# Sliding-window attention and a slotted MoE on one core: part of a weight read by the sync queue, and a request moved

## The chip, the cores and the metric

The kernel runs on one core of one Trainium2 chip. A time is the device time of one execution in microseconds. The kernel before was timed 13 times: the median is 183.29 us, the lowest 182.49 and the highest 183.64.

## The reference

Inputs are q, k and v of shape (8 batches, 8 heads, 576 positions, 64), and the MoE's `phi` (512 x 32), `w1` (8 experts, 512 x 1024) and `w2` (8 experts, 1024 x 512), all fp32. Two stages follow each other.

- Attention: scores are `q k^T / 8`. Heads 0 to 3 see the last 32 positions, heads 4 to 7 every fourth of the last 128 ("dilated"). After a softmax over the visible positions the result is multiplied by v. With the heads side by side this gives x, 4608 rows of 512.
- Soft MoE: `logits = x @ phi`. A softmax over the 4608 rows forms 32 slot inputs out of x, four for each expert. Every expert computes `relu(s @ w1) @ w2` on its four slots. A softmax over the 32 slots of each row mixes the 32 slot outputs into that row of the output, 4608 x 512 in fp32.

So w1 and w2 (16.8 MB each in fp32) are read once for 32 rows of work, q, k and v are 9.4 MB each, and the output is 9.4 MB.

## The kernel before

All tensors are computed in fp16. Every load and every store is a DMA issued by POOL (GpSimd), and the DMA converts: loads read fp32 and write fp16, stores read fp16 and write fp32. The order of the instructions of each engine is the program's order (`manual_schedule`), with no planner.

**The batches.** A prologue requests the first inputs and prepares masks. Then ten steps b = 0 to 9 follow, each made of `slot0`, `slot1` and `slot2`. Step b does the scores, exp and attention-times-v of batch b, transposes raw q and k of batch b+1 on DVE (`qk_plain`, L233, and `qk_dil`, L242), and finishes batch b-1: it transposes x (`back_xT_plain`, `back_xT_dil`) and computes the logits (`back_logits`, whose exp on ACT, L409, goes into the tile ET at columns 576 (b-1) and up). `back_erow` and `back_u` of batch b-2 add up the slot inputs.

**The loads.** Raw q and k of batch b+2 are requested in `slot0(b)` (`load_qk`, L132) and v of batch b+2 in `slot1(b)` (`load_v`, L146 for the first 512 positions and L149 for the last 64). `spread_v` copies part of v on DVE (L201) and part on POOL (L204, L208); it stands ahead of `load_v` in the order of POOL. Between these, `weights(b, g)` requests half an expert's w1 at a time (`load_w1(e, i)`, L212, 256 rows of 4 KB, 512 KB once converted) and near the end w2 (`load_w2`, L216 for experts 0 to 5). Experts 6 and 7 are read in halves of 256 columns (L224): first the left half of both, then the right half of both, eight DMAs in all.

**The tile ET** has 128 partitions and 4672 columns of fp16. It is set to zero in `slot0(0)` by DVE (L559), and column 576 b and up is written by ACT when batch b's logits are done, in `slot2(b+1)`. Columns from 2560 on are thus not used until `slot2(5)`.

**The prologue's order on POOL.** Raw q and k of batch 0 in two parts (four requests, L137), then five selects that build `ident` and `masks` (L483), `load_v(0)`, the select that builds `orders` (L493), `load_qk(0, 1)`, `load_qk(1, 1)`, `load_v(1)`, and phi (L505). On DVE the copy L506 waits for the masks and is followed by the first transposes of q and k.

**The end.** `slot_out(half, experts)` multiplies by w2 (L706) and copies 256 columns of slot outputs to `so_sb` (L714). `combine(half, pair)` makes 256 rows by 256 columns of output: two matmuls with ET (L722), a scaling by ACT in two passes (even pairs, L734) or by DVE in one (odd pairs, L738), and one store by POOL (L744). `combine_full(pair)` does 256 rows of all 512 columns (L755, L757, L761, stores L768). The order is: half 0 of w2 for all experts; eight pairs of half 0, with w2's half 1 of expert 6 after the sixth; half 1 of expert 7; then ten full pairs, with the eight pairs of half 1 between the last ones.

Of the kernel before, what the change touches and what calls it, by code (L numbers as in the profile page):

```python
# [44 lines left out]
NH = DMODEL // 2  # L45
# [4 lines left out]
def kernel(  # L50
# [75 lines left out]
    def load_qk(ti, b, groups=None):  # L126
        ten = (q, k)[ti]
        if (ti, b) not in raw:
            raw[(ti, b)] = raw_pool.tile([128, 2, PJ * D], FP16, name=f"raw{ti}_{b}", tag=f"raw{ti}")
        t = raw[(ti, b)]  # L130
        if groups is None:
            nc.gpsimd.dma_start(  # L132
                out=t, in_=ten[b].rearrange("(g h) (p j) d -> (h p) g (j d)", g=2, j=PJ)
            )
        else:
            for g in groups:
                nc.gpsimd.dma_start(  # L137
                    out=t[:, g, :],
                    in_=ten[b, 4 * g : 4 * g + 4].rearrange("h (p j) d -> (h p) (j d)", j=PJ),
                )  # L140

    def load_v(b):
        slab = fix.tile([128, V_SLAB], FP16, name=f"vs_{b}", tag=f"vs{b % 2}")
        sa, sb = (slab[:, 2048 * i : 2048 * i + 2048].rearrange("a (h n) -> a h n", h=H) for i in range(2))
        vstage[b] = (sa, sb)
        nc.gpsimd.dma_start(  # L146
            out=sa, in_=v[b, :, 0:512, :].rearrange("h (a r) d -> a h (r d)", r=DIL)
        )
        nc.gpsimd.dma_start(  # L149
            out=sb[0:LEFT], in_=v[b, :, 512:S, :].rearrange("h (a r) d -> a h (r d)", r=DIL)  # L150
        )
# [57 lines left out]

    def load_w1(e, i):  # L210
        src = moe_w1[e].rearrange("(c p) f -> p c f", p=128)
        nc.gpsimd.dma_start(out=w1t[e][:, 2 * i : 2 * i + 2, :], in_=src[:, 2 * i : 2 * i + 2, :])  # L212

    def load_w2(e, half=None):
        if half is None:
# [242 lines left out]
    def prologue():  # L458
        load_qk(0, 0, (0,))
        load_qk(1, 0, (0,))  # L460
        nc.vector.memset(masks, 0.0)
        nc.vector.memset(ones, 1.0)
        nc.vector.memset(orders[0:32], 1.0)
        for i in range(2):
            nc.vector.memset(kTp[i][:, S : S + 64, :], 0.0)
            nc.vector.memset(kTd[i][:, S : S + 80, :], 0.0)
            nc.vector.memset(qTd[i][:, S : S + 16, :], 0.0)
            nc.vector.memset(vP[i][:, :, :, D : D + 1], 1.0)
            nc.vector.memset(vP[i][TAIL:128, 4, :, :], 0.0)
            nc.vector.memset(vD[i][:, :, :, D : D + 1], 1.0)  # L470
            nc.vector.memset(vL[i][:, :, :, D : D + 1], 1.0)
        load_qk(0, 0, (1,))
        load_qk(1, 0, (1,))
        left = masks[:, W1:].rearrange("p (u c) -> p u c", c=LEFT)
        band = (
            (ident, ones, [[1, 128]], 0, -1, ALU.is_equal, 0.0),
            (masks[:, 0:WQ], masks[:, 0:WQ], [[1, WQ]], 0, -1, ALU.is_ge, MASKED),
            (masks[:, 0:WQ], masks[:, 0:WQ], [[-1, WQ]], WINDOW - 1, 1, ALU.is_ge, MASKED),
            (left, left, [[0, 5], [1, LEFT]], 32, -1, ALU.is_ge, MASKED),
            (left, left, [[0, 5], [-1, LEFT]], -1, 1, ALU.is_ge, MASKED),  # L480
        )
        for dst, src, pattern, base, mult, op, fill in band:
            nc.gpsimd.affine_select(  # L483
                out=dst,
                in_=src,
                pattern=pattern,
                base=base,
                channel_multiplier=mult,
                compare_op=op,
                fill=fill,  # L490
            )
        load_v(0)
        nc.gpsimd.affine_select(  # L493
            out=orders[0:32],
            in_=orders[0:32],
            pattern=[[-1, DIL], [1, 128]],
            base=0,
            channel_multiplier=-DIL,
            compare_op=ALU.is_equal,
            fill=0.0,  # L500
        )
        load_qk(0, 1)
        load_qk(1, 1)
        load_v(1)
        nc.gpsimd.dma_start(out=phi_raw, in_=moe_phi.rearrange("(p l) s -> p l s", l=4))  # L505
        nc.vector.tensor_copy(out=masks[:, WQ:W1], in_=masks[:, 0:TAIL])  # L506
        qk_plain(0, 0)
        qk_plain(1, 0)
        nc.vector.memset(emask, 1.0)
        for i in range(1, 4):  # L510
            nc.vector.tensor_copy(out=orders[32 * i : 32 * i + 32], in_=orders[0:32])
        for part in range(2):
            qk_dil(0, 0, part)
        qk_dil(1, 0, 0)
# [5 lines left out]
    def weights(b, g):  # L520
        if b < B - 2:
            if g == 1 or b > 0:
                load_w1(*next_w1.pop(0))
        elif b == B - 2:
            if g == 0:
                while next_w1:
                    load_w1(*next_w1.pop(0))
                load_w2(0)
                load_w2(1)
            else:  # L530
                slab_weights(4, "vs0", V_SLAB)
                load_w2(4)
        elif g == 0:
            raw_pool.release()
            pool = tc.alloc_tile_pool(name="w2b", bufs=1, side="right")
            late_pools.append(pool)
            for e in (2, 3):
                w2t[e] = pool.tile([128, 8, DMODEL], FP16, name=f"w2_{e}", tag=f"w2_{e}")
                load_w2(e)
        else:  # L540
            slab_weights(5, "vs1", V_SLAB)
            load_w2(5)
            slab_weights(6, "qk0", QK_SLAB)
            slab_weights(7, "v0", V_SLAB)
            for half in range(2):
                for e in HALVED:
                    load_w2(e, half)

    def slot0(b):
        att, b1, b2, b3 = b < B, b - 1 >= 0 and b <= B, 2 <= b < B + 2, b + 1 < B  # L550
        if att:
            qk_dil(1, b, 1)
            emit_scores(b, 0)
            if b + 2 < B:
                load_qk(0, b + 2)
                load_qk(1, b + 2)
            weights(b, 0)
        if b == 0:
            nc.vector.memset(ET, 0.0)  # L559
            nc.vector.memset(siTm, 0.0)  # L560
            nc.vector.tensor_reduce(
                out=halves, in_=orders[:, 0, 0:TAIL], axis=mybir.AxisListType.X, op=ALU.add
            )
            nc.vector.tensor_copy(
                out=emask[:, NE - 1, :], in_=halves.broadcast_to([128, N_SLOTS])
            )
        if b1:
            emit_av(b - 1, "d", 0)
            emit_norm(b - 1, "d", 0)
        if b2:  # L570
            back_erow(b - 2)
        if b1:
            emit_av(b - 1, "d", 1)
            emit_norm(b - 1, "d", 1)
            back_xT_plain(b - 1, 0)
        if att and b > 0:
            order_v_plain(b)
        if b == 1:
            order_phi()
        if b1:  # L580
            emit_av(b - 1, "d", 2)
            emit_norm(b - 1, "d", 2)
            back_xT_plain(b - 1, 1)
        if b2:
            back_u(b - 2)
# [129 lines left out]

    psum_f = tc.alloc_tile_pool(name="psum_f", bufs=4, space=bass.MemoryType.PSUM)

    def combine(half, pair):
        fp = psum_f.tile([128, 2, NH], FP32, name=f"f{half}_{pair}", tag="f")
        r0 = 256 * pair  # L720
        for k in range(2):
            nc.tensor.matmul(  # L722
                fp[:, k, :],
                ET[:, r0 + 128 * k : r0 + 128 * k + 128],
                so_sb[:, NH * half : NH * half + NH],
                start=True,
                stop=True,
                skip_group_check=True,
            )
        ot = out_pool.tile([128, 2, NH], FP16, name=f"ot{half}_{pair}", tag=f"ot{half}", bufs=NSPLIT // 2)  # L730
        if pair % 2 == 0:
            for k in range(2):
                blk = 2 * pair + k
                nc.scalar.activation(  # L734
                    out=ot[:, k, :], in_=fp[:, k, :], func=AF.Copy, scale=rrow[:, blk : blk + 1]
                )
        else:
            nc.vector.tensor_tensor(  # L738
                out=ot,
                in0=fp,  # L740
                in1=rrow[:, 2 * pair : 2 * pair + 2, None].broadcast_to([128, 2, NH]),
                op=ALU.mult,
            )
        nc.gpsimd.dma_start(  # L744
            out=out[r0 : r0 + 256, NH * half : NH * half + NH].rearrange("(k p) n -> p k n", k=2),
            in_=ot,
        )
# [74 lines left out]
```

## Time and profile before

| | |
|---|---|
| median of 13 executions | 183.29 us |
| profiled execution, its own time | 183.64 us |
| span in its trace (first to last instruction) | 181.9 us |
| PE busy | 144.2 us, 79% |
| DVE busy | 106.6 us, 59% |
| ACT busy | 90.7 us, 50% |
| POOL busy | 83.4 us, 46% |
| moved by DMA, counted at the destination | 40.75 MB, mean 224 GB/s |
| read from and written to HBM | 61.93 MB and 9.44 MB, 392 GB/s |

The span is divided by the page into 40 slices. PE is the busiest engine, and between 24 and 112 us its slices are nearly all at nine tenths; yet in the row of the DMA engines every slice but the first is at nine tenths too, to the very end. In the last 24 us only output is written. A line of the timeline gives start, duration, engine, source line, operation, and in brackets how long the engine had been idle and what ended that. Issuing instructions of DMAs are listed under POOL with the time that they hold POOL; the transfer itself comes later.

### The profile page before, as it was taken

What the parts mean: (1) busy time and instruction counts of PE and PEld (TensorE: products, weight loads), DVE (VectorE), ACT (ScalarE), POOL (GpSimd) and SP (SyncE); (2) the same over time, 40 slices, a digit from 0 to 9 for tenths busy, and PEclk for the clock granted to TensorE, in tenths of its full rate; (3) what the DMA queues carried; (4) which work ended last, traced back from release to release, by engine and by line L of the source; (5) the groups of instructions that cost most, each with busy time, mean ns of one, the idle gap of its engine ahead of it and who ended that gap; (6) DMA issues with size and microseconds to landing.
All of it is one profiled execution on the core that took longest, in us unless ns stands there. A gap on an engine that the chain in (4) does not pass through costs nothing.

```text
span 181.9 us, 5572 instructions
## 1 busy us (share of the span) xinstructions
PE 144.2 (79%) x2464; PEld 86.6 (48%) x2464; DVE 106.6 (59%) x231; ACT 90.7 (50%) x163; POOL 83.4 (46%) x117
## 2 busy tenths in 40 slices
PE   0557987999999999999999999999879475787000
PEld 0224544746646746746746746757344263232000
DVE  4788785676884984984984984536040202499100
ACT  2053365748566766766766766765201204698000
POOL 7953642633535345345283715621101110998830
PEclk9999998798799999999999999998556968799755
DMA  4999999999999999999999999999999999999997
GB/s 61 197 164 215 196 210 205 212 209 203 212 209 206 211 211 203 212 210 202 215 207 204 211 211 213 217 214 215 214 212 216 200 196 168 298 397 408 408 407 181
DMA packets 31303, 40.75 MB, mean 224 GB/s; under 512 B 1584, under 2 KB 18992, under 8 KB 31280
## 3 DMA queue, kind: packets, MB, share of 16 engines
q0 software_dynamic: 31280, 40.41, 119.4%
q8 instruction: 19, 0.31, 0.6%
q14 instruction: 4, 0.03, 0.0%
HBM read 61.93 MB, written 9.44 MB: 392 GB/s over the span
## 4 chain that ended last, share of the span: by engine, by line
PE 43%; DMA 32%; ACT 8%; issue 5%; POOL 4%; DVE 3%; POOLq 1%
DMA w<-in_moe_w_dram 23%; PE lg L405 8%; PE o_p L336 7%; PE sa L279 6%; ACT p L290 6%; DMA raw<-in_q_dram 5%; PE sa L268 5%; PE sb L268 4%; DMA out_dram<-of 4%; PE u L447 3%; PE rd L386 2%; PE vb L162 2%; PE va L162 2%; PE rp L374 2%; ACT of L757 1%
## 5 line engine op out<-in xcount | busy, mean ns | idle before, releaser
L290 ACT ACTIVATE p<-sa 128x960 f16<-128x960 f32 (+2 forms) x24 | 21.4, 891 | 31.3 <-PE sb L279 30.7
L336 PEld LDWEIGHTS <-p 128*128 128x128 f16 (+2 forms) x544 | 19.7, 99 | 12.8 <-issue 8.6
L242 DVE STREAM_TRANSPOSE qk<-raw 128x320 uint32<-128x320 uint32 (+1 forms) x32 | 21.6, 679 | 0.3
L233 DVE STREAM_TRANSPOSE qk<-raw 128x576 uint32<-128x576 uint32 x16 | 20.0, 1251 | 2.7 <-DMA raw<-in_q_dram 1.5
L290 ACT ACTIVATE p<-sb 128x960 f16<-128x960 f32 (+2 forms) x24 | 21.2, 885 | 0.0
L208 POOL COPY v<-v 32x1024 f16<-32x1024 f16 x8 | 8.3, 1036 | 27.9 <-DVE v L201 19.3
L268 PE MATMUL sa<-masks,ident 128*128 128x480 f16 (+2 forms) x48 | 14.5, 388 | 6.3 <-POOL masks L483 4.8
L405 PE MATMUL lg<-xTd,phi 128*128 128x288 f16 x32 | 18.3, 659 | 0.0
L279 PEld LDWEIGHTS <-qk 32*128 32x128 f16 x832 | 12.3, 98 | 12.3 <-issue 9.3
L279 PE MATMUL sa<-qk 32*128 32x160 f16 (+4 forms) x416 | 16.2, 215 | 2.0 <-DVE qk L233 1.9
L336 PE MATMUL o_p<-v,p 128*128 128x65 f16 (+1 forms) x288 | 16.7, 203 | 0.8 <-ACT v L171 0.7
L268 PEld LDWEIGHTS <-ident 128*128 128x128 f16 x96 | 9.2, 106 | 16.8 <-issue 7.3
L224 POOL DMA_DIRECT2D w<-in_moe_w_dram x8 | 6.0, 746 | 24.4 <-DMA w<-in_moe_w_dram 21.7
L279 PE MATMUL sb<-qk 32*128 32x160 f16 (+4 forms) x416 | 16.3, 215 | 0.0
L358 DVE TENSOR_TENSOR xd<-o_d,rc_d 128x448 f16<-128x448 f32 (+1 forms) x24 | 14.4, 602 | 0.8
L358 DVE TENSOR_TENSOR xp<-o_p,rc_p 128x448 f16<-128x448 f32 (+1 forms) x24 | 14.4, 602 | 0.8
L744 POOL DMA_DIRECT2D out_dram<-ot x16 | 11.5, 719 | 6.7 <-PE f L722 6.7
L268 PE MATMUL sb<-masks,ident 128*128 128x480 f16 (+2 forms) x48 | 14.4, 386 | 0.2 <-ACT p L290 0.2
L212 POOL DMA_DIRECT2D w<-in_moe_w_dram x16 | 11.6, 728 | 3.2 <-DMA w<-in_moe_w_dram 2.2
L162 PE MATMUL va<-vs,orders 32*128 32x256 f16 (+1 forms) x96 | 12.1, 289 | 1.0 <-ACT p L290 1.0
L409 ACT ACTIVATE ET<-lg 128x288 f16<-128x288 f32 x16 | 6.6, 411 | 12.2 <-PE lg L405 12.0
L738 DVE TENSOR_TENSOR ot<-f,rrow 128x512 f16<-128x512 f32 x8 | 5.5, 688 | 12.0 <-PE f L722 11.9
(97 smaller groups left out, 272.3 us busy)
## 6 DMA issues: line engine op xcount, KB each, us to landing
w<-in_moe_w_dram POOLq DMA_DIRECT2D x16, 512.0 KB, 14.6
w<-in_moe_w_dram POOLq DMA_DIRECT2D x6, 1024.0 KB, 26.5
out_dram<-of POOLq DMA_DIRECT2D x10, 512.0 KB, 6.0
vs<-in_v_dram POOLq DMA_DIRECT2D x8, 512.0 KB, 10.5
out_dram<-ot POOLq DMA_DIRECT2D x16, 256.0 KB, 4.3
raw<-in_q_dram POOLq DMA_DIRECT2D x7, 576.0 KB, 13.3
raw<-in_k_dram POOLq DMA_DIRECT2D x7, 576.0 KB, 13.4
w<-in_moe_w_dram POOLq DMA_DIRECT2D x8, 256.0 KB, 23.9
```

The source lines that it names most:

```text
L162: nc.tensor.matmul(o.rearrange("p (h d) -> p h d", h=4), l, st[:, 0:4, D * r : D * r + D], start=(r == 0), stop=(r == DIL - 1), skip_group ...
L208: nc.gpsimd.tensor_copy(out=vL[b % NV][0:32, :, :, 0:D], in_=vD[b % NV][96:128, :, :, 0:D])
L212: nc.gpsimd.dma_start(out=w1t[e][:, 2 * i : 2 * i + 2, :], in_=src[:, 2 * i : 2 * i + 2, :])
L233: nc.vector.transpose(out=dst, in_=src)
L242: nc.vector.transpose(out=o, in_=i)
L268: nc.tensor.matmul(sps[h // 2][:, h % 2, 0:n], ident, bias[g], start=True, stop=False, skip_group_check=True,)
L279: nc.tensor.matmul(sps[h // 2][:, h % 2, c0 : c0 + w], kt_[32 * h : 32 * h + 32, k0 : k0 + 128, tt], qt_[32 * h : 32 * h + 32, q0 : q0 + w ...
L290: nc.scalar.activation(out=pt, in_=sps[ab][:, :, 0:n], func=AF.Exp, scale=SCALE)
L336: nc.tensor.matmul(o[p0 : p0 + np_, n, :], l, rr, start=(k == 0), stop=(k == len(jobs) - 1), skip_group_check=True,)
L358: nc.vector.tensor_tensor(out=x.rearrange("p t (h d) -> p (t h) d", h=4)[0:nq, u0:u1, :], in0=o[0:nq, 0:n, 0:D], in1=rc[0:nq, 0:n, None].b ...
L405: nc.tensor.matmul(lp, phi4[:, kc].rearrange("p c s -> p (c s)"), rhs, start=(kc == 0), stop=(kc == 3))
L744: nc.gpsimd.dma_start(out=out[r0 : r0 + 256, NH * half : NH * half + NH].rearrange("(k p) n -> p k n", k=2), in_=ot,)
```

## The change

Four things are edited.

- `load_w1(3, 0)` leaves out rows 0 to 127 of expert 3's w1. These are read by 16 DMAs on the sync queue (SP), each of 8 rows, as fp32, into columns 2560 to 4607 of ET seen as fp32 (128 x 1024). They are issued in `slot0(3)`, after a memset of two columns by DVE (`side_load`).
- In `slot0(5)` POOL converts the 128 x 1024 values into w1's tile and sets the columns of ET to zero again (`side_cast`).
- In the prologue `load_v(0)` goes ahead of the five selects, and `load_qk(0, 1)` ahead of the select of `orders`.
- `combine(0, 0)` becomes two calls of the new `combine_one`, each for 128 rows with one matmul, one scaling (ACT for the first, DVE for the second) and one store.

```diff
     def load_w1(e, i):
         src = moe_w1[e].rearrange("(c p) f -> p c f", p=128)
-        nc.gpsimd.dma_start(out=w1t[e][:, 2 * i : 2 * i + 2, :], in_=src[:, 2 * i : 2 * i + 2, :])
+        c0 = 2 * i + (e == SIDE_E and i == 0)
+        nc.gpsimd.dma_start(out=w1t[e][:, c0 : 2 * i + 2, :], in_=src[:, c0 : 2 * i + 2, :])
+
+    SIDE_E, SIDE_C0 = 3, 2560
+    side = ET[:, SIDE_C0 : SIDE_C0 + 2048].bitcast(FP32)
+
+    def side_load():
+        nc.vector.memset(ET[:, SIDE_C0 : SIDE_C0 + 2], 0.0)
+        for p in range(0, 128, 8):
+            nc.sync.dma_start(out=side[p : p + 8], in_=moe_w1[SIDE_E, p : p + 8, :])
+
+    def side_cast():
+        nc.gpsimd.tensor_copy(out=w1t[SIDE_E][:, 0, :], in_=side)
+        nc.gpsimd.memset(ET[:, SIDE_C0 : SIDE_C0 + 2048], 0.0)
...
         load_qk(1, 0, (1,))
+        load_v(0)
         left = masks[:, W1:].rearrange("p (u c) -> p u c", c=LEFT)
...
-        load_v(0)
+        load_qk(0, 1)
         nc.gpsimd.affine_select(
...
-        load_qk(0, 1)
         load_qk(1, 1)
...
             weights(b, 0)
+        if b == 3:
+            side_load()
+        if b == 5:
+            side_cast()
...
+    def combine_one(half, blk):
+        fp = psum_f.tile([128, NH], FP32, name=f"f{half}_one{blk}", tag="f")
+        cols = slice(NH * half, NH * half + NH)
+        r0 = 128 * blk
+        nc.tensor.matmul(fp, ET[:, r0 : r0 + 128], so_sb[:, cols], start=True, stop=True)
+        ot = out_pool.tile([128, NH], FP16, name=f"oo{half}_{blk}", tag=f"oo{half}_{blk}")
+        if blk % 2 == 0:
+            nc.scalar.activation(out=ot, in_=fp, func=AF.Copy, scale=rrow[:, blk : blk + 1])
+        else:
+            nc.vector.tensor_scalar(
+                out=ot, in0=fp, scalar1=rrow[:, blk : blk + 1], scalar2=None, op0=ALU.mult
+            )
+        nc.gpsimd.dma_start(out=out[r0 : r0 + 128, cols], in_=ot)
+
     def combine(half, pair):
+        if half == 0 and pair == 0:
+            combine_one(half, 0)
+            combine_one(half, 1)
+            return
```

## The prediction

> **What bounds the kernel now.** I read the slices of the page first, then the queues, then the chain of waits, then the windows.
>
> ```profile
> DMA  4999999999999999999999999999999999999997
> GB/s 61 197 164 215 196 210 205 212 209 203 212 209 206 211 211 203 212 210 202 215 207 204 211 211 213 217 214 215 214 212 216 200 196 168 298 397 408 408 407 181
> ...
> q0 software_dynamic: 31280, 40.41, 119.4%
> ...
> HBM read 61.93 MB, written 9.44 MB: 392 GB/s over the span
> ```
>
> The DMA engines have packets in flight in every slice but the first; POOL's queue q0 carries everything. Bytes are counted at the destination: loads are written as fp16, so 210 GB/s there is 420 GB/s read. The bytes are fixed by the problem, so the span is start-up, bytes over rate, and the places where the rate falls. Four columns of the windows matter here: stretch, length, and at the end DMA share and GB/s.
>
> ```profile
> 9.00:13.00 4.00, 2.66 (x68) 1.18 (x56) 3.47 (x7) 1.83 (x2) 2.57 (x4) 1.00 1.22 155
> 104.00:108.00 4.00, 4.00 (x67) 2.31 (x67) 3.46 (x8) 3.01 (x6) 1.50 (x2) 1.00 1.12 210
> 148.00:152.00 4.00, 2.42 (x52) 1.77 (x43) 0.00 (x0) 0.00 (x0) 0.00 (x0) 0.77 1.45 196
> 152.00:156.00 4.00, 3.53 (x27) 1.94 (x27) 2.08 (x3) 2.73 (x7) 1.67 (x3) 0.66 1.02 149
> 156.00:160.00 4.00, 2.95 (x19) 1.21 (x18) 1.98 (x3) 2.72 (x6) 4.00 (x6) 0.92 1.81 363
> 168.00:172.00 4.00, 0.00 (x0) 0.00 (x0) 0.78 (x2) 0.00 (x0) 4.00 (x6) 0.79 1.64 408
> ```
>
> Two dips: v(0), at 9 to 13 us, and 152 to 156 us, where w2 runs out before the output begins. The end of the chain shows what waits there:
>
> ```profile
> 146.84 10.43 DMA w<-in_moe_w_dram
> 157.32 0.32 PE so L706 x4
> 157.66 0.38 ACT so_sb L714
> 158.08 0.39 PE f L755
> ```
>
> and the timeline shows the first output:
>
> ```profile
> 151.96 0.29 PE L706 MATMUL so<-w,hTm 128*32 128x256 f16 x4 [1.12 <-DMA w<-in_moe_w_dram]
> 152.30 0.37 ACT L714 CAST so_sb<-so 128x256 f16<-128x256 f32 x1 [9.30 <-PE so L706]
> 153.20 2.35 ACT L734 ACTIVATE ot<-f,rrow 128x256 f16<-128x256 f32 x6 [0.53 <-PE f L722]
> 154.33 5.72 POOL L744 DMA_DIRECT2D out_dram<-ot  x8 [6.75 <-PE f L722]
> ```
>
> [...] The trace records each packet, and every engine's 4-byte completion mark. For the last w2 DMA the marks run from 152.6 to 157.0 us: seven engines are done by 153.8, nine between 154.2 and 157.0; the means (153.1 and 155.4) are 2.3 us apart. Earlier the spread was the same kind (3.2 us at 112.6 us), and from 112 to 137 us nearly all engines step at the same 0.305 us per 8 KB read, so a lag, once there, stays. Early engines stand idle until the first store, which waits for the latest engine's share of expert 7's first half. From 154.33 POOL issues one store each 0.715 us without a pause, the 512 KB stores start when that row is done (160.05), and then 408 GB/s sets the end. So the end moves one for one with that latest engine.
>
> [...]
>
> **The side read.** w1(3,0) loses 128 rows. A w1 row is 4 KB read, and 508 such packets started in the 5 us from 104: 16 engines × 5 / 508 = 0.157 us each. Every engine loses 8 of its 16: −1.26 us. Added are 128 rows of 4 KB read and 4 KB written. The trace has no uncast load; output writes at 408 GB/s give 4096 / 25.5 = 0.161 us per packet. Sixteen per engine on 0 to 7: +2.57 us. Net +1.3 us for engines 0 to 7, −1.26 us for 8 to 15: the sum is nil, the relative shift 2.5 us, beside the 2.3 us of lag just measured.
>
> Which engines lag decides the sign, and no view names them. One hint: where two packets begin in the same nanosecond, the records list one first. From 155.6 to 157 us, of 30 such pairs of a store packet (an early engine) and a w2 packet (a late one), 27 list the store first; from 142 to 147 us the early engine is first in 7 of 8. If equal times stand in order of engine number, the late engines have high numbers. I take that, and that the change relieves them.
>
> Gain: at most 1.26 us at the latest engine (half 0: 151.6 to 150.4). The early seven, the last of which finish 3.2 us ahead of the latest, come up 1.3 us and stay below. But at least one of engines 0 to 7 belongs to the nine; if it is one of those 1.4 us behind the last, it becomes the latest after about 0.1 us of gain. I take 0.9; bounds 0 to 1.26.
>
> Bound from above on the cost: [...] From below it is nothing [...]. I take under 1 us, which the slack covers.
>
> **Its other instructions.** The DVE memset of 2 columns is some 0.07 us (the 128x16 memsets of L470), where DVE then idles 0.9 us (before 55.57); queued behind it are normalisations of batch 2. SP's 16 issues: SP has nothing else before the end. Raw tiles of batch 5, requested at 52.5 and 55.0 us, land 13 us later and are transposed at 74.0 and 76.2, so engines late by even 7 us there cost nothing. The w1 issue shrinks from 0.73 towards 0.56 us (128 rows, as L149), hidden.
>
> POOL's cast and memset stand at 83.8 us. L204's 1024 columns take 1.03 us and I take that for the cast; the 2048-column memset is 2.05 us at that pace, less if it is packed; 16 waits of 0.04 us (a semaphore event of L216) add up to 0.7. Together at most 3.8 us, and behind it are these:
>
> ```profile
> 83.79 1.03 POOL L204 COPY v<-vs 16x1024 f16<-16x1024 f16 x1
> 89.24 1.04 POOL L208 COPY v<-v 32x1024 f16<-32x1024 f16 x1 [4.43 <-DVE v L201]
> ```
>
> L208 waits 4.43 us for DVE: that hides it. Without the cover, v(7) would be requested later, and it is needed a batch later. ACT's exp of batch 4 into these columns comes after 91.7 us; the zeros are there by 88. Cost nil.
>
> **v(0) first.** Its two issues (0.94 + 0.56 us) go ahead of five masks selects: v(0) is requested 1.5 us earlier, masks end at 6.8 instead of 5.3, and DVE's copy L506, with the transposes behind it, starts 0.75 us later. DVE waits 0.74 us for raw at 16.79, which absorbs it; without that cover PE would start batch 1 up to 0.75 us late, still 20 us ahead of w2. q(1) is requested 0.6 us sooner, k(1) and v(1) keep their time. On the engines the order stays q, k, v(0), q, k. v(0)'s packets start at 8.75 us, behind k, 2 us after their request; asking sooner doesn't explain away the dip. Were it fixed, 155 would become 197 GB/s: 4 × 42 / 197 = 0.85 us. I take 0; bounds 0 and 0.85 gained.
>
> **combine_one.** Pair 0 of half 0 leaves in two stores. The first needs one ACT pass of 0.42 us instead of two: POOL starts at 153.9 instead of 154.33. Two issues of 0.56 replace one of 0.72, so pair 1 is issued at 153.9 + 1.12 = 155.0 against 155.05. Early engines start 0.5 us sooner, the row ends 0.05 us sooner. Gain 0.05.
>
> **Sum.** −0.9 −0.05 = −0.95 us on this execution (span 181.9, time 183.64, so 1.74 around it): span about 180.95, time 182.7. Its time is 0.35 above the median 183.29; on the median: 182.3.
>
> **Rivals.** (a) [...] Against: at load SBUF takes only half of what the engines read, and the engines run 3 us apart. It decides from about 1.9 us of extra time, where engines 0 to 7, up by 1.3, overtake the latest[...]. (b) *The late engines are 0 to 7.* The order of ties may mean nothing. Then +1.3 − 0.05: 184.5. (c) *It hides.* The 8 rows are spread over all engines after all, or a middle engine becomes the latest: 183.2. (d) *The dip at 9 us goes too:* 182.3 − 0.7 = 181.6.
>
> **Numbers.** Forecast 0.40, (d) 0.08, (c) 0.13, (a) 0.25, (b) 0.14. A difference below 0.2% (0.37 us) can't be told from none here. Faster 0.48, same 0.13, slower 0.39. The forecast's own range is 181.9 to 182.8; the range for 8 in 10 takes in (b), (c), (d) and the lower half of (a): 181.3 to 185.3.
>
> **What would show it.** Right: 149 GB/s at 152 to 156 rises, the first store is issued near 153 us, the last w2 lands near 156. The side rows show as 4 KB packets on an SP queue from about 55 us, landing within 10 us; POOL's L208 still waits on DVE after the cast. [...] side DMAs that take much longer than 10 us, a GB/s dip at 55 to 70 us, w2 later. (b): no dip there, w2 later by about 1.3. (d): 9 to 13 us near 197 GB/s. I am wrong altogether if the w2 landings don't move while the end does.

## The result and the profile after

| | before | after |
|---|---|---|
| median | 183.38 us (48 runs) | 185.12 us (11 runs, 184.49 to 186.00) |
| profiled execution, its own time | 183.64 us | 184.96 us |
| span in its trace | 181.9 us | 183.1 us |
| read from HBM, written | 61.93, 9.44 MB | 61.93, 9.44 MB |

The changed kernel is slower: 1.0096 of before, 95% interval 1.0079 to 1.0114, or +1.8 us where the forecast was −0.95. 185.12 lies inside the range of 181.3 to 185.3, but only because rivals (a) and (b) had been taken in; the forecast itself had the wrong sign. The two profiled executions that are compared below differ by 1.3 us, a little less than the medians.

The page of the changed kernel: slices of the DMA engines, queues, bytes.

```profile
DMA  4999999999999999999999999999999999999996
GB/s 63 194 190 213 200 207 205 214 204 206 213 206 206 229 217 207 212 182 189 212 211 159 200 211 214 215 215 217 210 215 215 208 195 199 328 395 410 406 409 160
...
q0 software_dynamic: 31168, 40.15, 118.0%
q1 hardware_dynamic: 256, 0.52, 1.2%
...
HBM read 61.93 MB, written 9.44 MB: 390 GB/s over the span
```

The queue q1 is new: 128 packets of 4 KB with their marks. The third slice, which holds v(0), is better than before (190 for 164), and so, taken together, are the two slices from about 146 to 155 us (195 and 199 for 196 and 168). Read by these two dips alone, the change works. The windows of the changed kernel (stretch, length, busy time of PE, weight load, DVE, ACT, POOL with counts, then granted clock, DMA share, GB/s; the share adds up the packets' times over the 16 engines, and passes 1 where an engine's packets overlap) say the same, and show two dips that before did not have. First the changed kernel:

```profile
9.00:13.00 4.00, 2.69 (x65) 1.32 (x60) 3.64 (x7) 1.83 (x2) 2.52 (x4) 1.00 1.31 184
80.00:82.00 2.00, 2.00 (x52) 1.18 (x48) 2.00 (x3) 1.86 (x6) 2.00 (x4) 1.00 0.87 162
96.00:98.00 2.00, 2.00 (x19) 0.98 (x17) 1.55 (x5) 1.55 (x3) 2.00 (x4) 1.00 0.90 137
152.00:156.00 4.00, 2.66 (x16) 1.71 (x15) 1.71 (x3) 1.89 (x5) 1.29 (x3) 0.73 1.44 197
```

The same two stretches in the kernel before:

```profile
80.00:82.00 2.00, 2.00 (x12) 0.61 (x14) 1.93 (x4) 0.41 (x1) 0.53 (x1) 1.00 1.14 207
96.00:98.00 2.00, 1.91 (x46) 1.34 (x36) 1.37 (x5) 1.76 (x3) 0.66 (x1) 1.00 1.38 201
```

152 to 156 us moves 197 GB/s for 149, as the prediction wanted, and yet the end is later, because the w2 in front of it comes later. The chain of waits shows the last w2 at 158.23 us (before 157.32):

```profile
120.55 26.92 DMA w<-in_moe_w_dram
147.47 0.28 issue
147.76 10.43 DMA w<-in_moe_w_dram
158.23 0.32 PE so L723 x4
158.57 0.38 ACT so_sb L731
```

and the timeline of the changed kernel the outputs:

```profile
153.21 0.37 ACT L731 CAST so_sb<-so 128x256 f16<-128x256 f32 x1 [6.12 <-PE so L723]
154.71 1.09 POOL L747 DMA_DIRECT2D out_dram<-oo  x2 [6.21 <-DVE oo L744]
155.79 5.01 POOL L779 DMA_DIRECT2D out_dram<-ot  x7
160.91 2.15 POOL L803 DMA_DIRECT2D out_dram<-of  x3
```

`so_sb` comes at 153.21 (before 152.30), the first store at 154.71 (154.33), the first 512 KB store at 160.91 (160.05): +0.9 us from half 0 of w2 to the row of stores, as w2 goes.

The packet records show what no view groups. Of the last w2 DMAs' 512-byte packets, the first engine to begin does so at 144.94 us (before 141.94), the last packet starts at 157.82 (156.88). The first engine came 3.0 us later, the latest 0.9 later. The prediction had +1.3 for the engines with side rows and up to −1.26 for the others: the spread did shrink, but on a base about 2 us too late. Some of that base is the two new dips of this one execution. In it PE ran at half clock for 6.8 us around 30 us and 6.8 us around 48 us (before 3.4 each) and for 3.4 us more at 62 and 76 us, and POOL, which waits for PE's results, reached its sixth L208 at 93.31 us (before 89.24), with the requests behind it. Whether that is the cause of +1.8 in general is one of the questions below. The side read itself began when planned, on the sync queue:

```profile
56.52 9.73 SPq L221 DMA_DIRECT2D ET<-in_moe_w_dram  x16
```

Its packets start between 59.9 and 70.7 us and take 233 ns on average (up to 493), where 172 ns is the unhindered value, that of the first 28. The first 32 begin in four groups of eight with the same spacing, 0.52 us apart (59.89 to 60.15, 60.41 to 60.66, 60.92 to 61.18, 61.44 to 61.69), and a mark of 4 bytes follows each packet, so eight engines take one row each of these DMAs. Which eight they are no record says. The prediction's "engines 0 to 7" is the author's assumption; below they are also called the eight.

### The profile page after: what moved, and what is told of

The parts are those of the page before. It is cut to its first block, busy times and chain, and to the rows that moved or that the text cites. A ratio compares the mean times of both kernels' runs of the same rounds, so it can differ in the third digit from the quotient of the medians.

```text
span 183.1 us, 5612 instructions
## 1 busy us (share of the span) xinstructions
PE 146.5 (80%) x2464; PEld 87.6 (48%) x2464; DVE 106.7 (58%) x233; ACT 90.6 (50%) x162; POOL 86.0 (47%) x120
## 3 DMA queue, kind: packets, MB, share of 16 engines
HBM read 61.93 MB, written 9.44 MB: 390 GB/s over the span
## 4 chain that ended last, share of the span: by engine, by line
PE 46%; DMA 20%; ACT 11%; DVE 6%; issue 5%; POOL 5%; POOLq 1%; DVEq 0%
DMA w<-in_moe_w_dram 20%; PE lg L418 8%; ACT p L303 7%; PE o_p L349 6%; PE sa L292 6%; PE sb L281 5%; PE sa L281 5%; PE rd L399 3%; PE u L460 3%; PE vb L162 2%; PE va L162 2%; DVE qk L255 2%; PE rp L387 2%; ACT of L792 2%; PE o_d L349 1%
## 5 line engine op out<-in xcount | busy, mean ns | idle before, releaser
L281 PE MATMUL sa<-masks,ident 128*128 128x480 f16 (+2 forms) x48 | 15.7, 416 | 7.3 <-POOL masks L497 6.2
L208 POOL COPY v<-v 32x1024 f16<-32x1024 f16 x8 | 8.3, 1036 | 26.5 <-PE sb L292 13.8
L292 PEld LDWEIGHTS <-qk 32*128 32x128 f16 x832 | 12.8, 101 | 12.0 <-issue 10.2
L292 PE MATMUL sa<-qk 32*128 32x160 f16 (+4 forms) x416 | 16.7, 219 | 0.8 <-DVE qk L246 0.7
L237 POOL DMA_DIRECT2D w<-in_moe_w_dram x8 | 6.0, 746 | 21.3 <-DMA w<-in_moe_w_dram 20.5
L281 PE MATMUL sb<-masks,ident 128*128 128x480 f16 (+2 forms) x48 | 15.4, 410 | 0.5 <-ACT p L303 0.5
L370 DVE RECIPROCAL rc_p<-o_p 128x7 f32<-128x7 f32 (+1 forms) x24 | 4.7, 197 | 13.0 <-PE o_p L349 12.5
L132 POOL DMA_DIRECT2D raw<-in_q_dram x7 | 5.0, 720 | 14.4 <-DVE qk L255 12.0
L392 ACT COPY xTp<-rp 128x576 f16<-128x576 f16 x16 | 10.4, 647 | 2.2 <-PE rp L387 2.2
```

The lines of the kernel that those rows point to most:

```text
L208: nc.gpsimd.tensor_copy(out=vL[b % NV][0:32, :, :, 0:D], in_=vD[b % NV][96:128, :, :, 0:D])
L281: nc.tensor.matmul(sps[h // 2][:, h % 2, 0:n], ident, bias[g], start=True, stop=False, skip_group_check=True,)
L292: nc.tensor.matmul(sps[h // 2][:, h % 2, c0 : c0 + w], kt_[32 * h : 32 * h + 32, k0 : k0 + 128, tt], qt_[32 * h : 32 * h + 32, q0 : q0 + w ...
L392: nc.scalar.copy(out=xTp_t[b][:, c, :], in_=rg)
```

## The experiments

The rivals stand against each other as follows. **Neighbours** (rival (a), theory C in the expectations): eight engines that carry 8 neighbouring rows at a time hold one another up, and the cost goes away when the same engines carry rows that lie apart. **Skew** (theory D): 16 more packets on each of the eight engines make one of them the latest, neighbours or not. **Clock and dry spells:** the side read has nothing to do with it, PE is late, and requests with it. **Parts:** the moved v(0) or `combine_one` cost the time. Every ratio is to the kernel before on the same chip.

**One part at a time.** The prologue alone:

```diff
+        load_v(0)            # ahead of the five selects
...
-        load_v(0)
+        load_qk(0, 1)        # ahead of the select of orders
```

> Only load_v(0) and load_qk(0, 1) are moved in the prologue. Theory A (PE is granted half clock more often in the batches, PE gets late, requests come late, the DMA engines run dry): the move fills the DMA dip at 9 to 13 us (155 to about 184 GB/s, as in the changed kernel) and the engines, now ahead, wait for PE; whether the kernel is slower follows the number of half-clock stretches before 112 us, 2 in the kernel before and 6 in the changed one. About 184.5 us if this edit alone brings more of them, 182.7 us if it brings none. Theory B (the side read costs): 182.7 us, faster by 0.6.

Measured: 182.87 us, 0.9976 (0.9957 to 0.9995). Windows and timeline of this kernel:

```profile
9.00:13.00 4.00, 2.70 (x67) 1.32 (x60) 3.64 (x7) 1.83 (x2) 2.52 (x4) 1.00 1.35 193
...
151.03 0.37 ACT L714 CAST so_sb<-so 128x256 f16<-128x256 f32 x1 [7.03 <-PE so L706]
153.27 5.71 POOL L744 DMA_DIRECT2D out_dram<-ot  x8 [7.05 <-ACT ot L734]
...
158.98 2.14 POOL L768 DMA_DIRECT2D out_dram<-of  x3
```

193 GB/s for 155 in the kernel before, and the whole tail about 1.1 us earlier in this execution. The packet records say how: v(0)'s 1152 packets of 512 bytes start at 8.8 us in both kernels, but the last starts at 12.61 instead of 13.59 us; the DMA share of the stretch 9 to 10 us is 1.30 instead of 0.95. So the first packet does not start earlier; what changed is that the engines no longer run empty between these packets. By the medians the part is worth −0.44 us (0.0024 x 183.58).

The side read alone, with `load_w1`, `side_load` and `side_cast` as in the change and nothing else:

```diff
+        if b == 3:
+            side_load()
+        if b == 5:
+            side_cast()
```

> Only the side read on the sync queue with its cast. Theory A: 182.3 to 182.5 us if the half-clock stretches stay at 2, since the late engines are relieved (152 to 156 us near 197 GB/s); about 184 if there are 5 or 6. Theory B (the side read itself costs, by its requests, its cast or its DMAs): about 185 us.

Measured: 185.94 us, 1.0138 (1.0084 to 1.0192). Here the dip at 152 to 156 us stays, and the next window is also low (before: 363):

```profile
152.00:156.00 4.00, 2.20 (x28) 1.32 (x21) 0.22 (x1) 0.82 (x3) 0.00 (x0) 0.83 1.14 156
156.00:160.00 4.00, 2.97 (x25) 1.09 (x23) 2.45 (x4) 2.69 (x8) 3.32 (x5) 0.60 1.09 207
```

```profile
154.65 0.37 ACT L731 CAST so_sb<-so 128x256 f16<-128x256 f32 x1 [11.55 <-PE so L723]
156.68 5.71 POOL L761 DMA_DIRECT2D out_dram<-ot  x8 [6.73 <-ACT ot L751]
```

The first store is 2.35 us later than before, the last 512-byte w2 packet starts at 159.23. Side packets take 283 ns on average. PE was as fast as before here (the fifth L208 at 75.52 us, before 75.58; half clock in the same two places), and of all 2-us windows from 14 to 142 us only the one at 66, where side packets are, is below 190 GB/s (180): the trace has the loss without the half clock. The order in which tied packets are listed, which the prediction took as a hint on engine numbers, turns over as well (at 142 to 147 us the late engine stands first in 14 of 19 ties, before the early one in 7 of 8). If the hint is good, engines that were early are now the late ones; that is not shown.

`combine_one` alone:

```diff
+        if half == 0 and pair == 0:
+            combine_one(half, 0)
+            combine_one(half, 1)
+            return
```

> Only the first pair's store is split. Theory A and theory B: within 0.2 us of the kernel before; nothing before 152 us is changed. If it is 0.5 us or more slower, the split store is a third cause.

Measured: 183.87 us, 1.003 (1.0012 to 1.0049): a small loss of 0.55 us. Its two stores hold POOL for 1.08 us, and the row behind them is 5.00 us, so pair 1 follows as computed:

```profile
151.43 0.37 ACT L714 CAST so_sb<-so 128x256 f16<-128x256 f32 x1 [6.53 <-PE so L706]
153.03 1.08 POOL L730 DMA_DIRECT2D out_dram<-oo  x2 [6.30 <-DVE oo L727]
154.11 5.00 POOL L762 DMA_DIRECT2D out_dram<-ot  x7
```

From `so_sb` to the first store it is 1.60 us, in before 2.03, which is what was meant. Its profiled execution took 183.12 us, the lowest of its 21, so it doesn't show where the median loses; that stays open.

**One DMA or sixteen.** The side read as one DMA of 128 rows, which takes all 16 engines (q1 has 144 packets here, 128 rows and 16 marks):

```diff
-        for p in range(0, 128, 8):
-            nc.sync.dma_start(out=side[p : p + 8], in_=moe_w1[SIDE_E, p : p + 8, :])
+        nc.sync.dma_start(out=side, in_=moe_w1[SIDE_E, 0:128, :])
```

> As the side read alone, but as one DMA of 128 rows instead of 16 DMAs of 8. If the 16 DMAs load only the early half of the engines, this one loads all 16 alike, the late engines keep their 1.3 us, and the dip at 152 to 156 us stays near 149 GB/s: 183.3 us, about 0.9 us above the side read with 8 rows if nothing else differs. Theory B, with the cost in the 16 small DMAs: 183.3 where the side read alone is at 185.

Measured: 183.61 us, 1.0009 (0.999 to 1.0028). Packets 174 ns on average, all begun between 58.5 and 62.3 us. The second queue, the cast, the memset and the shorter w1 request together cost at most 0.5 us by this interval, and nothing that can be told from none, and 152 to 156 us stays at 150 GB/s.

The whole change with that one DMA in place of the 16:

> The changed kernel with its side read as one DMA of 128 rows. If the 16 DMAs of 8 neighbouring rows are what made the changed kernel slower (theories C and D), 183.0 to 183.4 us: the 0.4 of v(0) first, and up to 0.5 lost by the split store. If the loss lies in the edits together (PE at half clock more often), 184.5 or more.

Measured: 183.41 us, 1.0001 (0.9978 to 1.0023). Between this and the changed kernel only the 16 small DMAs differ, and the difference is 0.0095, 1.7 us: the whole loss. This also answers the clock. The profiled execution of this kernel (184.11 us, clock 0.87) has the half-clocked stretch at 60 us, POOL's sixth L208 at 91.62 us, and low windows at 82 to 86 and 96 to 98 us (169 to 175 and 163 GB/s, though with DMA shares of 1.14 to 1.32, so not as dry as in the changed kernel), and the median is still that of before. The clocks of the single executions say it more plainly: the four of the changed kernel with a mean clock of 0.89 or more took 184.49 to 185.51 us, while the 27 such executions of the kernel before, among those timed beside the single parts, have a median of 183.54 and none over 184.27. At an equal clock the loss is there, so the clock is not what the change added.

16 rows in each of eight DMAs, so that all 16 engines take part, as the author assumes:

```diff
+        for p in range(0, 128, 16):
+            nc.sync.dma_start(out=side[p : p + 16], in_=moe_w1[SIDE_E, p : p + 16, :])
```

> The side read alone as 8 DMAs of 16 neighbouring rows: all 16 engines carry the same share[...]. Theory C: packets take longer than 172 ns here too and all engines lose a little, about 184 us; theory D: the shares are even, so 183.5 us as with one DMA of 128 rows.

Measured: 185.28 us, 1.008 (1.0051 to 1.0109), above both values that were expected. By that assumption no engine gets more than another here, and still +1.5 us. Side packets take 333 ns, and the packets of POOL's queue that start between 60 and 68 us grow too: those of 2304 bytes from 193 to 206 ns, those of 2048 from 173 to 217. Windows of this kernel:

```profile
60.00:62.00 2.00, 1.58 (x63) 1.11 (x61) 1.68 (x3) 0.42 (x1) 0.26 (x1) 1.00 1.38 180
62.00:64.00 2.00, 2.00 (x48) 1.32 (x46) 1.87 (x4) 2.00 (x6) 2.00 (x3) 1.00 1.48 171
```

The DMA share rises to 1.38 and 1.48 (before: 1.13 and 1.09) while the rate falls to 180 and 171 GB/s (before: 216 and 209): packets are in flight and stand. That is a stall, and if the shares are even, one without any skew.

**Rows that lie apart.** Each DMA still has 8 rows, but every fourth row:

```diff
-        for p in range(0, 128, 8):
-            nc.sync.dma_start(out=side[p : p + 8], in_=moe_w1[SIDE_E, p : p + 8, :])
+        for j in range(4):
+            for s in range(4):
+                p = 32 * j + s
+                nc.sync.dma_start(out=side[p : p + 29 : 4], in_=moe_w1[SIDE_E, p : p + 29 : 4, :])
```

> The side read alone, again as 16 DMAs of 8 rows on the same engines, but the 8 rows of a DMA are every fourth one of 32 instead of 8 neighbours[...]. Theory C ([...] a side packet took 283 ns on average with 8 neighbours against 174 ns with one DMA of 128 rows, and the low engines come out late): packets near 172 ns, the low engines only 1.3 us up, the late engines relieved; 182.3 to 183.3 us, where 8 neighbours gave 185.9. Theory D (shifting bytes onto half the engines is itself too much): no change against 8 neighbours, about 185.5 us.

> v(0) requested first, and the side read with rows four apart; no split store. Theory C: both gains add up, 181.8 to 182.6 us, below v(0) first alone (182.9). Theory D: 185 us.

Measured: 192.42 us, 1.0437 (1.0386 to 1.0488), and with the prologue's move 190.76, 1.0317. Both are spoiled by a wait that the edit brought in. Timeline of the first:

```profile
64.12 0.29 PE L430 MATMUL ep<-ident,ET 32*128 32x32 f16 x5 [6.50 <-DMA ET<-in_moe_w_dram]
```

PE reads other columns of ET, and with strided rows in the DMA it waited 6.5 us for the side read (6.57 us in the second kernel; with neighbouring rows no such wait is listed). The packets were at 172 ns, but the times say nothing on neighbours. So the side read got a tile of its own, first with neighbouring rows:

```diff
-    side = ET[:, SIDE_C0 : SIDE_C0 + 2048].bitcast(FP32)
+    side = consts.tile([128, FDIM], FP32, name="side")
...
-        nc.gpsimd.memset(ET[:, SIDE_C0 : SIDE_C0 + 2048], 0.0)
```

> The side read alone with 8 neighbouring rows in each of 16 DMAs, into a tile of its own instead of ET (so no zeroing by POOL, and no other access can be made to wait for it). Theories C and D: like the side read into ET, 185 to 186 us. If it is below 184, ET was the cause.

Measured: 186.61 us, 1.0151 (1.0114 to 1.0187), packets 251 ns on average. ET and its memset are not the cause. Then the same tile with every fourth row, alone and with the prologue's move:

> The same with rows four apart[...], now without the wait of PE for ET (6.5 us) that made the first trial of it unreadable. Theory C [...]: packets at 172 ns, the low engines only 1.3 us up, the late ones relieved: 182.3 to 183.3 us. Theory D (2.6 us more on half the engines is too much in any case): as with neighbouring rows, 185 to 186.

> v(0) requested first, and the side read with rows four apart into its own tile. Theory C: 181.8 to 182.6 us, faster than both kernels. Theory D: 184.5 to 185.5.

Measured: 184.42 us, 1.0047 (1.0024 to 1.0069), packets 173 ns; and 183.71, 1.0006 (0.9975 to 1.0036). Own tile, eight neighbours, against own tile, eight rows apart, is the clean pair: as many DMAs of as many rows, the same bytes, 1.0104 between them, 1.9 us (by the two intervals, some 1.1 to 2.7). That is the price of neighbouring rows, two thirds of the side read's loss. 184.42 lies between the two values that were expected for the rows apart, and meets neither. What is left, +0.86 us, has unhindered packets, and is the opposite of the gain that the prediction expected. The order of tied packets at 142 to 147 us goes the same way: with neighbours the late engine stands first in 16 of 18 ties, with rows apart in 3 of 15.

One question stays open: with every fourth row the DMA also reads rows of w1 in HBM that lie apart, where it read 32 KB in one piece. Every run here changes both ends together, so whether neighbours stall where SBUF is written or where HBM is read is not shown.

**What is left.** Half of the rows: eight DMAs, 64 rows, while the other 64 stay on POOL's queue as a DMA of their own.

```diff
+        if c0 > 2 * i:
+            nc.gpsimd.dma_start(out=w1t[e][64:128, 0, :], in_=src[64:128, 0, :])
...
-        for j in range(4):
+        for j in range(2):
```

> As the side read into its own tile with rows four apart, but for 64 of the 128 rows only: 8 side DMAs, the other 64 rows stay on POOL's queue as a DMA of their own (one more issue). The full one gave 1.0047 of before. If engines 0 to 7 hold one of the latest at the end already, so that each row moved to them adds to the end, about half of that loss: 1.0023 (184.0 us). If the full one moved too much and the latest are engines 8 to 15, relieved by 0.63 us: 183.0 or below (0.997). If the loss is a fixed cost of a second queue and its many small DMAs, also near 1.002, but with the last w2 multiplication where it was before. Side packets at 172 ns in all cases.

Measured: 183.82 us against 183.73, 0.9996 (0.9965 to 1.0026). Half of it costs nothing and gains nothing that can be measured.

If one of the eight engines is the latest by itself, giving it side rows was the mistake. Seven rows in each DMA leave one of the eight out, called engine 7 in the expectations; that the seven rows go to the other seven, and that the one left out is the latest, is a guess of the author's. 16 rows stay on POOL's queue:

```diff
-                p = 32 * j + s
-                nc.sync.dma_start(out=side[p : p + 29 : 4], in_=moe_w1[SIDE_E, p : p + 29 : 4, :])
+                p = 28 * j + s
+                nc.sync.dma_start(out=side[p : p + 25 : 4], in_=moe_w1[SIDE_E, p : p + 25 : 4, :])
```

> The side read into its own tile, rows four apart, but seven rows in each of the 16 DMAs (112 rows), and 16 rows stay on POOL's queue as a DMA of their own. Seven rows go to engines 0 to 6, so engine 7 gets none and loses 7 of its w1 rows, as 8 to 15 do (1.1 us less); 0 to 6 get 16 x 0.172 - 1.1 = 1.65 us more. [...] If the latest of engines 0 to 6 are as late as engine 7: as with eight rows, 1.005. If the loss is a fixed cost of 16 small DMAs: 1.005 too, but with a balanced end.

> The same with v(0) requested ahead of the selects, which alone gave 0.9976. [...] Otherwise 1.002.

Measured: 184.78 us, 1.0047 (1.0022 to 1.0073), and with the prologue's move 184.15, 1.0011 (0.9984 to 1.0038). The loss is that of eight rows: leaving one engine out does not help, since, if the guess on the seven holds, another engine that has side rows ends as late. That engine 7 by itself is the latest is hard to hold: half of the rows would then have moved the end by +0.75 us, and the interval there ends at +0.5. Last, the 16 DMAs aimed at fewer engines, by the same assumption: four rows each (64 rows), then two (32 rows), the rest on POOL's queue.

```diff
+                p = 16 * j + s
+                nc.sync.dma_start(out=side[p : p + 13 : 4], in_=moe_w1[SIDE_E, p : p + 13 : 4, :])
```

> 16 side DMAs of four rows, four apart, into their own tile (64 rows; the other 64 stay on POOL's queue as a DMA of their own): engines 0 to 3 get 16 x 0.172 - 0.63 = 2.1 us more, all others 0.63 us less. If the latest two are among 0 to 3: up to 2 us later, ratio 1.008 to 1.011. If they are among 4 to 6: near 0.998, unless engines 0 to 3 end within 2 us of them. If 16 small DMAs cost by themselves: 1.005.

> The same with two rows in each of the 16 DMAs (32 rows; the other 96 stay): engines 0 and 1 get 16 x 0.172 - 0.31 = 2.4 us more, all others 0.31 us less. If the latest two are 0 and 1: 1.012 and a pair of engines at the end 2.4 us further out. If they are among 2 to 6: 0.998 to 1.005, as far behind as 0 and 1 come. If 16 small DMAs cost by themselves: 1.005.

Measured: four rows 183.62 us, 0.9995 (0.9974 to 1.0017); two rows 184.15, 1.0029 (1.0005 to 1.0053). Four rows in 16 DMAs cost at most 0.3 us by their interval, so it is not 16 small DMAs on a second queue that cost by themselves. A reading that fits is that it matters which engines get the packets. The engine numbers in it are labels for an assumption of the author's, that DMAs of n rows always go to the same n engines, 0 to n − 1, one row each; no record here names an engine. The table sets what each group of engines gets (16 or 8 packets of 0.172 us, less 0.157 for each w1 packet moved away from the engine) beside the median's move, the ratio less one, times 183.6:

| kernel | side rows to | these get | the others | measured |
|---|---|---|---|---|
| half of the rows | 0 to 7 | +0.75 us | −0.63 us | −0.07 |
| eight rows apart | 0 to 7 | +1.50 | −1.26 | +0.86 |
| seven rows apart | 0 to 6 | +1.65 | −1.10 | +0.86 |
| four rows apart | 0 to 3 | +2.12 | −0.63 | −0.09 |
| two rows apart | 0 and 1 | +2.44 | −0.31 | +0.53 |

All five fit one picture, within their intervals: the latest engine is none of 0 to 6; the latest of 4 to 6 ends about 0.7 us before it, and the latest of 0 to 3 about 2.0 us before it. Then the end moves by the largest of what the groups come to: half +0.05 (0.75 − 0.7), eight rows +0.8, seven +0.95, four +0.1 (2.12 − 2.0), two +0.4. The two positions were fitted to five medians, so this is an argument and not a sight of the engines. A cost that grows with the number of rows would fit as well but for the last line, whose interval (0.1 to 1.0) begins close to nothing. The count of engines with w2 packets in flight, from the number of 512-byte packets that begin in half a microsecond (0.042 us each), goes with the picture: with eight and with seven rows two engines are alone at the end until 157.5 us and later, with half of the rows until 157.0, as in the kernel before, and with four rows no two stand behind the others; all are done by 156.3.

The same sum, with the packet length of each trace in place of 0.172 us, gives an estimate for runs to which it was not fitted. Eight neighbouring rows in ET: 16 × 0.283 − 1.26 − 0.7 = +2.6 us (measured +2.5); in their own tile, at 0.251, +2.1 (+2.8, interval 2.1 to 3.4). Sixteen neighbouring rows, eight packets on every engine if the shares are even: 8 × 0.333 − 1.26 = +1.4 (+1.5); one DMA of 128 rows, at 0.174, +0.1 (+0.2). So longer packets on the engines that carry the side rows, and little room before these become the latest, are enough for the sizes measured.

## Why the prediction was wrong

Two terms of the prediction's sum failed, and both concern engines 0 to 7.

The first is the room that it gave them. "I take 0.9" at the latest engine, with engines 0 to 7 up by 1.3 us, needs each of these to end at least 2.2 us ahead of it. With rows apart the packets are unhindered (172 ns), so that no stall is left in the time, and the side read still costs +0.86 us instead of gaining 0.9. The room that fits the runs is about 0.7 us, for a relative shift of 2.8.

The second is the stall: "I take under 1 us, which the slack covers", an estimate that no measurement stood behind. The clean pair measured 1.9 us, the very value from which the prediction's rival (a) was to decide, though rival (a) reckoned with a slack of 3.2 us for all of engines 0 to 7. The packets show the size: 233 ns on average in the changed kernel, 251 and 283 in the two side reads alone, for 172; times 16 packets this is 1.0, 1.3 and 1.8 us more on each of the engines that carry them. So the stall was at or above what the prediction took, and no slack covered it.

What spoke for "under 1" was that SBUF takes in half of what the engines read, and that the engines run 3 us apart. The first does not hold for the side read itself, which is not converted, so that its 4 KB are written whole (packets of 4096 bytes at the destination). The second kept no stall away in the runs. And the prediction left out that a side write that stalls may also hold POOL's packets. Two traces of loads agree, with 2048-byte packets of POOL's queue at 203 ns (eight neighbours in ET, alone) and 217 ns (16 neighbours) for 173; in the changed kernel's own trace they stay at 173, so there only the side packets themselves are seen to be longer.

Point by point:

- **What bounds the kernel: right, as far as is seen.** DMA, and the end follows the latest engine's w2: in the side read alone the last w2 packet starts 2.35 us later than before and so does the first store.
- **Eight rows go to engines 0 to 7: the count agrees with the runs.** q1 has 256 packets for 16 DMAs, 8 of data and 8 marks each, and seven rows leave seven. That these engines are numbers 0 to 7 was assumed; no record names them.
- **The skew, −0.9: wrong, though the latest engine may be where it was put.** The prediction took the latest engine among the high numbers, which the picture above keeps, from a hint that no run confirmed. It knew that one of engines 0 to 7 belongs to the late nine, named the case that this one stands 1.4 us behind the last and leaves a gain of 0.1, and still took 0.9. The fit puts it at 0.7, and the shift at +1.5: +0.8, where +0.86 was measured. What should have been done is to take the end as the larger of two numbers, the low engines' and the high engines', and see that the shift of 2.5 us was larger than any gap it could close.
- **Cast, memset and w1 issue, nil: right.** In the timeline of the changed kernel L208 still waits for DVE behind them, as foretold, now 1.47 us instead of 4.43:

```profile
87.86 1.03 POOL L224 CAST w<-ET 128x1024 f16<-128x1024 f32 x1
88.95 1.80 POOL L225 MEMSET ET<- 128x2048 f16 x1
90.82 1.03 POOL L204 COPY v<-vs 16x1024 f16<-16x1024 f16 x1
93.31 1.04 POOL L208 COPY v<-v 32x1024 f16<-32x1024 f16 x1 [1.47 <-DVE v L201]
```

  1.03 and 1.80 us for the 1.03 and at most 2.05 forecast, and the single DMA of 128 rows, which carries the same cast, is at 1.0009.
- **v(0) first, 0 taken of 0 to 0.85: within its bounds, but the value was wrong.** "Asking sooner doesn't explain away the dip" came from the start of v(0)'s first packet, and that start did not move. What moved was how densely they follow. The window's DMA share, 0.95 in the microsecond from 9, would have said that engines ran empty. Rival (d) had this step, with 0.7 for the 0.44 measured, but its time needed the rest to be right too.
- **combine_one, −0.05:** measured +0.55 (0.2 to 0.9); each store's issue takes 0.54 us where 0.56 was forecast, and why the median loses is open.
- **The sum.** The side read alone +2.53, v(0) −0.44, `combine_one` +0.55 make +2.6, where the change has +1.8. The interval of the side read alone (+1.5 to +3.5) covers the gap; put on top of the other two edits its 16 DMAs cost 1.7. Its packets were also shorter there, 233 ns for 283, which times 16 is 0.8 us; one execution of each can't say whether that is the reason.
- **Signs to look for.** 149 GB/s at 152 to 156 did rise, to 197, in the changed kernel's trace, and stood for nothing: the stretch was fuller because the work had slid into it. A rate in a fixed window is a sign only together with the time at which the work ends. "Side DMAs that take much longer than 10 us" was a bad sign too: the stall was 16 times 0.06 to 0.11 us, and had to be read from the packets.

The moved request of v(0) alone, 0.9976, is the best of all the kernels run here, ahead of both the kernel before and the changed one.

## What to carry to other kernels

Here a load of eight rows was carried by eight engines (eight marks for each DMA, where one of 128 rows has 16), and, by the fit, whatever else these engines carried paid for it. A load of all 128 rows in one DMA cost nothing that could be measured (1.0009); rows that lie apart were cheaper than neighbours (by 1.9 us), but not free (+0.86 us). Where small loads can't be avoided, read the packets' length, not the DMA's. Before shifting work between engines in parallel, write down the end of each group after the shift; the gain is at most the gap between the latest and the next group, and here it was, by the fit, 0.7 us for a shift of 2.8. Where the engines run empty for want of requests (here a DMA share of 0.95 beside 109 GB/s, from 9 to 10 us), an earlier request can help though the first packet starts no sooner (1.30 and 174 GB/s).

## What the runs showed of the hardware

- Eight neighbouring fp32 rows of 4 KB in each of 16 DMAs: 233 to 283 ns per packet on average, up to 511; sixteen neighbouring rows in each of eight DMAs 333 ns; every fourth row 172 to 178 ns in nine traces; one DMA of 128 rows 174 ns. Neighbours against every fourth row, at both ends of the DMA, is 1.9 us for 512 KB.
- While such a read runs, the packets of the other queue can be longer too: for 2048 bytes 203 ns (eight neighbours in ET, alone), 182 (in their own tile) and 217 (16 neighbours), where before has 173. In the changed kernel they stayed at 173.
- The sync queue gave out 16 small DMAs in 9.3 to 12.4 us. With neighbouring rows it waited for earlier ones to land in between, 4.4 us in eight waits in the changed kernel; with eight rows apart no such wait is listed, and it took 10.8 us all the same. One DMA of 128 rows was through in 3.8 us from its first packet to its last.
